# One joined product of the spectral convolution is summed as two again, and the list of jobs is laid out anew

## The chip, the cores and the metric

The kernel runs on one core of a Trainium2 chip. The core has a matmul engine (TensorE, PE in the profile), a vector engine (VectorE, DVE), an activation engine (ScalarE, ACT), a general engine (GpSimd, POOL), and a queue engine that issues transfers (SyncE, SP). Each engine works through its own instructions in program order and waits on semaphores for the others. The metric is the device time of one execution in microseconds (us); a time of several runs is their median.

## The reference

Two independent computations share the kernel. Half A is attention in a sliding, dilated window over 2048 positions, width 576, 32 heads of 18 channels, 8 keys per position with a distance of 2. Half B is a gated long convolution: a short filter over four taps of k, times v, then a causal convolution of length 2048 with one filter per channel, then times q.

```python
qkv = (x @ wqkv).reshape(B, S, 3, H, Dh)                  # A
logits = einsum("bhsd,bhswd->bhsw", q, k[idx]) * scale
o = einsum("bhsw,bhswd->bhsd", softmax(logits), v[idx])
a = o.reshape(B, S, D) @ wo
kv = (sum over t of k_pad[:, t:t+S] * shift_k[:, ks-1-t]) * v      # B
y = irfft(rfft(kv, 2S) * rfft(ssm_k, 2S))[:, :S] + kv * ssm_D
b = q * y
out = concatenate([a, b], axis=-1)
```

## The kernel before

Half B cuts the 2048 positions into four blocks of 512. Each block of kv (xw in the profile) and of the filter (Ks) is turned into a spectrum by matmuls with sine tables (jobs `x...`, line 682, and `K...`, lines 567 and 568). Output block j is the sum over i of 0 to j of the spectrum of input block i times the spectrum of filter block j - i. The channels are worked in thirds t of 192. A complex product is made in three real products on VectorE (job `pjti`, line 950, one instruction over 128 x 2304 elements) into one of five homes (`PHOMES`), and TensorE adds the products of one (j, t) up with identity matrices into PSUM (job `zjti`, line 975, sixteen 64 x 64 matmuls of 384 columns, in two accumulators r of eight). After the last term ScalarE copies both accumulators out (line 988); for the very last sum one of the two copies is VectorE's (line 986).

The signs with which TensorE adds depend on m = j - i alone, and those of m and m + 2 are opposite. For the thirds listed in `JOINED` a job `yjti` (line 958) therefore subtracts the product of i + 2 from that of i on VectorE, and the sum of i + 2 does not exist:

```python
gone = [(j, t, i + 2) for j, t, i in joined]
def join_products(n):
    tt(product_home(n), product_home(n), product_home(n + 2), ALU.subtract)
...
    if (j, t, i) not in gone:
        job(f"z{j}{t}{i}", spectral_sum, n)
    if (j, t, i) in joined:
        job(f"y{j}{t}{i}", join_products, n)
```

Then the inverse transform (jobs `i...`, line 1010; `b...` turns halves around, line 1059; the last piece of block 3, columns 384 to 575, is `i3384L`, lines 1029 and 1038), the gate by q (jobs `g...`, lines 1020 and 1075) and the store.

Half A has the projections (`q`, `k`, `v` jobs with unit numbers, lines 322 to 355, two parts a and b), the window's products (`L...`, VectorE, line 706) summed over a head's channels by TensorE (`G...`, line 720), the softmax (`sm...`), its weights spread by transfers (`D...`), times v (`V...`, VectorE, line 813), summed by TensorE (`A...`, lines 824 and 838), and the output projection (`O...`, lines 880 and 888).

Other names: `T` are the taps of a block (VectorE), `M` folds kv (line 545), `F` folds a filter block (line 602, copied out at line 605), `I` and `X5` small transposes (lines 397 and 428), `S1` and `Ex` work of ScalarE alone, `RG` copies of the weights of v (line 780), `N` one-row filter instructions on VectorE, `Tk3` forms the third part of filter block 3 by a transfer on SP and then an adding transfer on POOL (lines 634 and 626). Its target is the home of product `p212`, so it waits for `z212`, and `p300` waits for it.

The order of all of this is written out by hand: `ORDER` is a list of job names, and each engine sees its part of the jobs in this order. A quote mark at a name turns the parts of a job around, so that its small matmuls come first. Matmul results live in four pairs of PSUM banks (`banks`), handed out in turn and given back after the copy; the products of VectorE live in three homes for `L` and for `V` (`LHOMES`, `VHOMES`) and the five for `p`. A job that finds its bank pair or its home still in use waits.

The matmuls have five shapes on the array: 128 x 128 (most), 64 x 64 (`z`, `b`, `A` and the small matmuls of `O`), 64 x 128 (the small matmuls of the projections), 128 x 64 (`M`, `I`, `X5`, the units with last digit 4) and 128 x 32 (`G`). How often the shape changes along TensorE's row follows from the list.

Of the kernel before, what the change touches and what calls it, by code (L numbers as in the profile page):

```python
# [17 lines left out]
PSUM = bass.MemoryType.PSUM  # L18

ORDER = """  # L20
    T0 k03a' T1 S1 k03b I1 k02a k02b Lk2 Lv2 I0 k00a' Lk3 Lv3 M01 X5 k00b q10a Ex q10b Lf3 T2 Lo3 q13a' q13b
    k10a k10b T3 k13a' Lf2 k13b q12a q12b N2 Lo2 k01a M10 k01b Lf1 M00 k11a k11b q11a M11 q11b Lf0 N3 Lw SV L001
    k12a M20 k12b x001 M21 x021 q24a x020 q24b x000 Lo1 k24a Fr Lo0 Z2 N1 RG3 k24b RG2 F3 RG0 F2 L000 K310 G000
    K311 K210 K211 L002 K313 G001 RG4 F1 G002 L003 G003 K302 L004 G004 K301 L010 K212 L011 K303 K213 K203 N0 F0
    L012 K200 K300 G010 L013 K201 K312 K202 RG1 G011 G012 K113 K103 G013 L014 G014 K112 K102 K101 L100 K100 K010
    K111 K110 sm0a K001 K013 sm0b v24a' L101 v24b L102 G100 L103 G101 K012 sm0c sm0d U3 U2 K000 K011 K003 G102
    K002 D0 D1 v11a v11b G103 L104 G104 ak00 M30 v12a' v12b ak02 v01a ak01 L110 G110 M31 L111 G111 v01b v00a'
    L112 G112 L113 Wl v00b G113 x031 U1 L114 G114 V04 v10a' v10b A04 sm1a sm1b v02a v02b v03a' sm1c v03b x201
    V10 V11 sm1d V12 A10 v13a' v13b D2 x330 x310 x301 V13 A11 V20 V21 x200 x331 x230 x010 x221 A20 x321 V22 x210
    x011 V23 D3 V34 ax02 x220 x030 x300 D4 A21 V40 V41 A34 D5 O000' x211 V42 x320 x231 x111 x131 Tx2 A40 V43  # L30
    x120 x101 ax00 x130 ax01 V50 x121 x311 O001 A41 V51 O100' p000 x100 x110 O010 A50 V52 z000 O011' V53 O101
    A51 Tk2 p010 z010 ax10 O020' O021 p020 z020 O110' ak10 i000 p200 i02880 Q0 p100 z100 p101 p110 p111 Q1 z101
    i02881 i001 p121 p120 O111 z110 p201 z111 z120 p210 z121 O120 p211 z200 z210 z211 p212 z212 z201 p202 z202
    Tx3 p220 Tk3 p221 O030' p222 O121 b0288 z220 p301 z221 O031' p302 b00 z222 p303 i200 i100 g0 Q2 p300 y300
    p312 i12880 i201 i101 i12881 z300 z301 z303 p310 p311 y310 O130 b10 b1288 p313 g1 Q3 p322 O131' z310 p320
    z311 p321 z313 i22880 i300 b20 y320 p323 i22881 i301 b2288 g2 z320 z321 z323 b30 i3384L g30 g3384
"""

LHOMES = (0, 1, 2, 0, 1, 2, 0, 1, 2, 0, 1, 2, 0, 1, 0, 1, 0, 1, 0, 1)
VHOMES = (0, 1, 2, 0, 1, 2, 0, 1, 2, 0, 1, 2, 0, 1, 2, 0, 1, 2)  # L40
OHOMES = (0, 1, 1, 0, 2, 0, 1, 0)
JOINED = ("300 310 320").split()
PHOMES = (0, 1, 2, 3, 0, 1, 2, 3, 0, 4, 1, 2, 3, 0, 4, 1, 2, 3, 0, 1, 2, 3, 0, 1, 2, 3, 0, 1, 2, 3)


# [6 lines left out]
def kernel(  # L52
# [900 lines left out]
    acc = {}  # L953
    joined = [tuple(map(int, name)) for name in JOINED]
    gone = [(j, t, i + 2) for j, t, i in joined]
# [180 lines left out]
```

## Time and profile before

| | |
|---|---|
| median of three runs | 206.78 us (206.28, 206.78, 206.79) |
| the profiled execution | 206.3 us, with a span of 204.6 us |
| TensorE busy | 196.9 us (96%) |
| VectorE busy | 192.3 us (94%) |
| ScalarE busy | 155.6 us (76%) |
| granted clock of TensorE, mean | 0.994 |

The span runs from the first to the last instruction; 1.7 us of the time lie around it. A group in the profile names line, engine, instruction, target and sources, and gives the count, the busy time, the mean duration and the idle time before. "PE busy" of matmuls is drawn from modelled ends and covers short stalls; where a stall matters, the starts of matmuls are compared.

### The profile page before, as it was taken

Reading aid. Unit: us, or ns where it says so; the run is one execution under the profiler, and the core shown is the slowest. Engines: PE = TensorE matmul, PEld = TensorE weight load, DVE = VectorE, ACT = ScalarE, POOL = GpSimd, SP = SyncE. Lnnn points to the kernel's source line nnn. Section 1 sums busy time; section 2 is a strip of 40 time slices with the busy share of each in tenths; the row PEclk is TensorE's granted clock in tenths of the full one; section 3 lists DMA queues with packets and bytes.
Section 4 is the critical chain, followed back from the end, with each engine's and each line's share of the span. In section 5 each row is a group of like instructions: output and inputs, shape, how many; then the busy total and the mean of one; then the engine's idle time right before and its main releaser. Section 6 shows DMA issues by size and latency. Waiting matters only on the chain.

```text
span 204.6 us, 5004 instructions
## 1 busy us (share of the span) xinstructions
PE 196.9 (96%) x2074; PEld 109.9 (54%) x2074; DVE 192.3 (94%) x146; ACT 155.6 (76%) x223; POOL 60.8 (30%) x106
## 2 busy tenths in 40 slices
PE   7999999999989999999999999999999999999990
PEld 2543544334455646543245556776666767766660
DVE  7559999999999999999999999999999999899992
ACT  4788995678899999966578678886778767767760
POOL 8989500011348581400380000004090001030300
PEclk9999999999999999999999999999999999999997
DMA  6999899989509869999899990879989303944555
GB/s 197 280 293 306 175 289 373 214 177 281 169 3 146 111 82 185 167 180 222 157 235 216 248 244 34 141 183 334 186 227 233 100 28 122 227 130 145 153 182 150
DMA packets 34916, 38.48 MB, mean 188 GB/s; under 512 B 17523, under 2 KB 28911, under 8 KB 34894
## 3 DMA queue, kind: packets, MB, share of 16 engines
q1 hardware_dynamic: 26668, 24.29, 46.5%
q0 software_dynamic: 5760, 11.36, 29.5%
q10 hardware_dynamic: 2466, 2.51, 3.6%
q8 instruction: 16, 0.26, 0.5%
q14 instruction: 6, 0.05, 0.1%
HBM read 13.11 MB, written 4.72 MB: 87 GB/s over the span
## 4 chain that ended last, share of the span: by engine, by line
PE 88%; DMA 3%; ACT 2%; DVE 2%; issue 1%; SPq 1%; DVEq 0%
PE ps_proj L322 18%; PE ps_fx L682 8%; PE ps_wo L888 8%; PE ps_z L975 8%; PE ps_inv L1010 7%; PE ps_acc L824 7%; PE ps_fk L567 5%; PE ps_log L720 5%; DMA Ks<-in_A_x_dram 3%; PE ps_proj L333 3%; PE ps_proj L326 3%; PE ps_proj L439 3%; PE ps_fk L568 3%; PE ps_fold L545 2%; PE ps_wo L880 1%
## 5 line engine op out<-in xcount | busy, mean ns | idle before, releaser
L322 PE MATMUL ps_proj<-xw 128*128 128x512 bf16 x160 | 38.5, 380 | 0.0
L706 DVE TENSOR_TENSOR av<-qk 128x4096 bf16<-128x4096 bf16 (+1 forms) x16 | 31.7, 2014 | 0.1
L322 PEld LDWEIGHTS <-xw 128*128 128x128 bf16 x160 | 13.9, 98 | 19.4 <-issue 5.7
L988 ACT ACTIVATE av<-ps_z 128x768 bf16<-128x768 f32 x23 | 17.2, 811 | 6.5 <-PE ps_z L975 6.0
L517 DVE TENSOR_TENSOR tB<-kj,skb 128x4608 bf16<-128x4608 bf16 (+1 forms) x8 | 19.3, 2416 | 0.1
L950 DVE TENSOR_TENSOR qk<-xw,Ks 128x2304 bf16<-128x2304 bf16 x14 | 18.9, 1354 | 0.3 <-PE ps_z L975 0.3
L684 ACT ACTIVATE xw<-ps_fx 128x576 bf16<-128x576 f32 x32 | 18.6, 665 | 0.3 <-PE ps_fx L682 0.2
L618 ACT ACTIVATE Ks<-ps_fk 128x576 bf16<-128x576 f32 x32 | 18.6, 699 | 0.2 <-PE ps_fk L568 0.2
L355 ACT ACTIVATE qk<-ps_proj 128x1024 bf16<-128x1024 f32 x14 | 14.3, 1023 | 5.2 <-PE ps_proj L333 2.8
L888 PE MATMUL ps_wo<-qk 128*128 128x288 bf16 x128 | 17.9, 287 | 0.0
L626 POOL DMA_DIRECT2D Ks<-Ks x8 | 10.1, 1426 | 26.0 <-PE ps_back L1059 19.3
L682 PE MATMUL ps_fx<-xw,TB 128*128 128x288 bf16 x128 | 17.7, 287 | 0.0
L567 PE MATMUL ps_fk<-Ks,TB 128*128 128x384 bf16 x62 | 16.5, 327 | 0.1
L824 PE MATMUL ps_acc<-av,ident 64*64 64x512 bf16 x160 | 15.3, 378 | 0.0
L1010 PE MATMUL ps_inv<-av,TI 128*128 128x288 bf16 (+1 forms) x112 | 15.2, 292 | 0.0
L568 PE MATMUL ps_fk<-Ks,TB 128*128 128x192 bf16 x62 | 15.2, 246 | 0.0
L682 PEld LDWEIGHTS <-TB 128*128 128x128 bf16 x128 | 11.9, 98 | 5.9 <-issue 2.7
L888 PEld LDWEIGHTS <-qk 128*128 128x128 bf16 x128 | 11.7, 98 | 5.4 <-issue 2.7
L355 ACT ACTIVATE v<-ps_proj 128x1024 bf16<-128x1024 f32 x9 | 9.3, 1033 | 6.5 <-PE ps_proj L322 4.5
L813 DVE TENSOR_TENSOR av<-Ks,v 128x4096 bf16<-128x4096 bf16 x6 | 13.5, 2286 | 0.0
L827 ACT ACTIVATE qk<-ps_acc 128x1024 bf16<-128x1024 f32 x8 | 8.2, 1024 | 6.7 <-PE ps_acc L824 6.7
L1010 PEld LDWEIGHTS <-TI 128*128 128x128 bf16 x112 | 10.6, 98 | 4.2 <-issue 1.1
(195 smaller groups left out, 441.6 us busy)
## 6 DMA issues: line engine op xcount, KB each, us to landing
Ks<-Ks POOLq DMA_DIRECT2D x8, 576.0 KB, 7.8
TB<-av SPq DMA_DIRECT2D x12, 256.0 KB, 5.4
kj<-in_B_k_dram SPq DMA_DIRECT2D x6, 504.0 KB, 7.0
vt<-in_B_v_dram SPq DMA_DIRECT2D x8, 288.0 KB, 5.3
Ks<-av SPq DMA_DIRECT2D x8, 256.0 KB, 5.6
out_dram<-qk ACTq DMA_DIRECT2D x5, 288.0 KB, 3.7
Ks<-in_A_x_dram SPq DMA_DIRECT2D x2, 576.0 KB, 5.4
xw<-in_A_wqkv_dram SPq DMA_DIRECT2D x2, 576.0 KB, 6.2
```

Of the source, the lines that this page charges most:

```text
L322: nc.tensor.matmul(ps[:, jp, :], wq(kb, comp, 128 * ct, 128), xT(kb, 1024 * jj + 512 * jp, 512), **se)
L355: nc.scalar.activation(view(t, o + pad + 1024 * jj, [[512, 2], [1, 512]]), ps[:], ACT.Copy)
L517: tt(to, view(kj, row * D, [[D, n], [D, 4], [1, D]]), view(skb, row * D, [[D, n], [0, 4], [1, D]]), ALU.mult)
L567: nc.tensor.matmul(o[:, 0:2], w, rhs[:, 0:2], start=start, stop=stop)
L568: nc.tensor.matmul(o[:, 2], w, rhs[:, 2], start=start, stop=stop)
L618: nc.scalar.activation(view(Ks, k_at(m, cs ^ (m & 1)) + 96 * gi, [[768, 3], [384, 2], [1, 96]]), acc3(ps), ACT.Copy, scale=(PSG, MSG)[cs][ ...
L682: nc.tensor.matmul(ps[:, pm, 0:HD], TX[:, 2 * pm + c, 128 * gi:128 * gi + 128], kv[:, 2 * c + pm, HD * h:HD * h + HD], start=(c == 0), sto ...
L706: tt(view(P, at, [[step, 4], [256, nj], [1, 256]]), view(t, o + 256 * hh, [[0, 4], [512, nj], [1, 256]]), view(tk, ok + 2 + 8 * ug + 256 * ...
L824: nc.tensor.matmul(acc[64 * o:64 * o + 64, h, :], ident[64 * h:64 * h + 64, 64 * h:64 * h + 64], view(P[s], 256 * u, [[2048, 2], [1, 256]] ...
L888: nc.tensor.matmul(ps[:, r, 0:HD], oT(hh, j + 2 * r, t)[:, o:o + 128], wo[:, t // 2, t % 2, HD * h:HD * h + HD], start=(t == 0 and not fli ...
L950: tt(product_home(n), view(xw, HB * XG[i] + QTR * t, [[HB, 3], [1, QTR]]), view(Ks, k_at(j - i, 0) + QTR * t, [[HB, 3], [1, QTR]]), ALU.mult)
L1010: nc.tensor.matmul(ps[:, c, 0:n], TI[:, sl, pm, 128 * c:128 * c + 128], Yall(j % 2, pm, sl, slice(c0, c0 + n)), start=(pm == 0 and sl == 0 ...
```

## The change

`JOINED` loses its third entry. In the last third (t = 2) of output block 3 there is no job `y320` any more; instead the sum `z322` is a job of its own. `ORDER` is written anew from end to end: the same jobs otherwise, in other places, with the quote marks at other names. Homes and everything else stay.

```diff
--- before.py
+++ after.py
@@ -18,28 +18,28 @@
 PSUM = bass.MemoryType.PSUM
 
 ORDER = """
-    T0 k03a' T1 S1 k03b I1 k02a k02b Lk2 Lv2 I0 k00a' Lk3 Lv3 M01 X5 k00b q10a Ex q10b Lf3 T2 Lo3 q13a' q13b
-    k10a k10b T3 k13a' Lf2 k13b q12a q12b N2 Lo2 k01a M10 k01b Lf1 M00 k11a k11b q11a M11 q11b Lf0 N3 Lw SV L001
-    k12a M20 k12b x001 M21 x021 q24a x020 q24b x000 Lo1 k24a Fr Lo0 Z2 N1 RG3 k24b RG2 F3 RG0 F2 L000 K310 G000
-    K311 K210 K211 L002 K313 G001 RG4 F1 G002 L003 G003 K302 L004 G004 K301 L010 K212 L011 K303 K213 K203 N0 F0
-    L012 K200 K300 G010 L013 K201 K312 K202 RG1 G011 G012 K113 K103 G013 L014 G014 K112 K102 K101 L100 K100 K010
-    K111 K110 sm0a K001 K013 sm0b v24a' L101 v24b L102 G100 L103 G101 K012 sm0c sm0d U3 U2 K000 K011 K003 G102
-    K002 D0 D1 v11a v11b G103 L104 G104 ak00 M30 v12a' v12b ak02 v01a ak01 L110 G110 M31 L111 G111 v01b v00a'
-    L112 G112 L113 Wl v00b G113 x031 U1 L114 G114 V04 v10a' v10b A04 sm1a sm1b v02a v02b v03a' sm1c v03b x201
-    V10 V11 sm1d V12 A10 v13a' v13b D2 x330 x310 x301 V13 A11 V20 V21 x200 x331 x230 x010 x221 A20 x321 V22 x210
-    x011 V23 D3 V34 ax02 x220 x030 x300 D4 A21 V40 V41 A34 D5 O000' x211 V42 x320 x231 x111 x131 Tx2 A40 V43
-    x120 x101 ax00 x130 ax01 V50 x121 x311 O001 A41 V51 O100' p000 x100 x110 O010 A50 V52 z000 O011' V53 O101
-    A51 Tk2 p010 z010 ax10 O020' O021 p020 z020 O110' ak10 i000 p200 i02880 Q0 p100 z100 p101 p110 p111 Q1 z101
-    i02881 i001 p121 p120 O111 z110 p201 z111 z120 p210 z121 O120 p211 z200 z210 z211 p212 z212 z201 p202 z202
-    Tx3 p220 Tk3 p221 O030' p222 O121 b0288 z220 p301 z221 O031' p302 b00 z222 p303 i200 i100 g0 Q2 p300 y300
-    p312 i12880 i201 i101 i12881 z300 z301 z303 p310 p311 y310 O130 b10 b1288 p313 g1 Q3 p322 O131' z310 p320
-    z311 p321 z313 i22880 i300 b20 y320 p323 i22881 i301 b2288 g2 z320 z321 z323 b30 i3384L g30 g3384
+    T0 k03a k00a k00b S1 Lk2 k03b k01a' k01b I0 Lv2 M00 X5 T1 Lk3 T2 Lv3 T3 I1 Lf3 Lo3 Lf2 q24a Lo2 N3 N2 Ex
+    q10a q10b k11a' k11b Lf1 q13a' q13b k12a' k12b q11a' q11b M01 q24b M11 k02a k02b M10 SV k13a k10a' k13b M20
+    k10b L000 q12a' q12b Lf0 x001 L001 x020 Lo1 x021 M21 x000 Lw RG2 RG3 Lo0 Fr k24a' N1 k24b Z2 F3 F2 K312 K310
+    K211 L002 K212 RG4 G000 G001 K311 L003 RG0 N0 G002 L004 L010 K313 F1 G003 K301 G004 L012 L011 K302 K210 K203
+    K200 K300 K303 F0 G010 K213 K201 K202 L013 G011 L014 G012 RG1 K111 K110 G013 G014 K103 L100 K101 K102 K112
+    K011 K010 K113 sm0a sm0b L101 L102 K100 v24a v24b G100 G101 L103 K013 sm0c sm0d K001 G102 L104 K012 K002
+    K003 K000 ak00 ak01 U3 U2 v00a' G103 L110 G104 L111 x031 v00b v01a v12a v01b ak02 G110 G111 L112 L113 v11a'
+    v11b Wl v12b G112 D0 L114 M31 G113 V04 x010 G114 sm1a v10a D1 v10b V11 A04 V10 sm1b v02a v02b v03a' sm1c
+    v03b x220 x201 sm1d V12 x211 A10 M30 V13 D2 V20 U1 v13a' v13b A11 V21 x301 D3 x311 x331 V22 x330 x011 A20
+    V23 x300 x230 x321 x310 x210 D4 V34 A21 V41 x030 V40 x231 D5 A34 V42 x320 x200 x221 x120 x130 x100 A40 V43
+    Tx2 O000' x111 x110 O001 ax02 Tk2 A41 ax00 O100' ax01 x131 x121 V50 x101 O010 V51 A50 p000 z000 V52 O011'
+    O101 V53 A51 p010 Q0 z010 ax10 O020' O021 p020 z020 ak10 p200 Q1 p100 O110' i000 i02880 z100 p101 z101 p111
+    i001 p120 p110 i02881 O111 z110 z111 z120 p121 z121 p201 p210 p211 O120' Tx3 z200 p212 z210 z211 z212 Tk3
+    p202 z201 p220 z202 p221 p222 O030' O121 b00 z220 p301 z221 z222 O031' b0288 p302 p303 i100 g0 i12880 p300
+    i200 i101 i201 Q2 i12881 y300 z300 b10 p312 p310 z301 b1288 p311 z303 b20 O130' O131 y310 z310 z311 p313
+    z313 g1 Q3 p323 i22880 p321 i300 i22881 i301 p320 p322 z320 b2288 g2 z321 z322 z323 b30 i3384L g30 g3384
 """
 
 LHOMES = (0, 1, 2, 0, 1, 2, 0, 1, 2, 0, 1, 2, 0, 1, 0, 1, 0, 1, 0, 1)
 VHOMES = (0, 1, 2, 0, 1, 2, 0, 1, 2, 0, 1, 2, 0, 1, 2, 0, 1, 2)
 OHOMES = (0, 1, 1, 0, 2, 0, 1, 0)
-JOINED = ("300 310 320").split()
+JOINED = ("300 310").split()
 PHOMES = (0, 1, 2, 3, 0, 1, 2, 3, 0, 4, 1, 2, 3, 0, 4, 1, 2, 3, 0, 1, 2, 3, 0, 1, 2, 3, 0, 1, 2, 3)
 
 
```

## The prediction

> **What bounds the kernel now.** I read the busy shares and the chain of the page first, then busy time by stage, then the starts on the VectorE row.
>
> ```profile
> span 204.6 us, 5004 instructions
> PE 196.9 (96%) x2074; PEld 109.9 (54%) x2074; DVE 192.3 (94%) x146; ACT 155.6 (76%) x223; POOL 60.8 (30%) x106
> ...
> PE 88%; DMA 3%; ACT 2%; DVE 2%; issue 1%; SPq 1%; DVEq 0%
> ```
>
> TensorE and VectorE are both nearly full, and the chain that ended last runs over TensorE. The table by stage (columns: busy us of PE, PEld, DVE, ACT, POOL, each with its count, then clock, DMA share and GB/s):
>
> ```profile
> 17.80:58.80 41.00, 41.00 (x291) 18.30 (x291) 40.27 (x27) 33.17 (x45) 9.39 (x19) 1.00 0.93 225
> 58.80:88.40 29.60, 28.84 (x279) 16.43 (x278) 29.46 (x20) 29.51 (x47) 16.90 (x16) 1.00 0.82 127
> 88.40:167.60 79.20, 79.03 (x954) 46.21 (x952) 78.72 (x53) 58.14 (x83) 13.54 (x17) 1.00 0.82 189
> 167.60:197.40 29.80, 29.53 (x437) 20.07 (x437) 28.65 (x23) 21.14 (x32) 5.13 (x7) 1.00 0.53 151
> ```
>
> From 17.8 on no stage has a free engine among these two: VectorE lacks 0.5 us of 79.2 in the third row, TensorE 0.2. From 58.8 to 88.4 (the filter units `K`) ScalarE is full as well, 29.51 of 29.60. Only the last row leaves VectorE 1.15 us. Where these waits are:
>
> ```profile
> 162.24 1.36 DVE L950 TENSOR_TENSOR v<-xw,Ks 128x2304 bf16<-128x2304 bf16 x1 [0.21 <-PE ps_z L975]
> ...
> 169.13 1.36 DVE L950 TENSOR_TENSOR v<-xw,Ks 128x2304 bf16<-128x2304 bf16 x1 [0.33 <-PE ps_z L975]
> ...
> 176.00 1.36 DVE L950 TENSOR_TENSOR qk<-xw,Ks 128x2304 bf16<-128x2304 bf16 x1 [0.25 <-PE ps_z L975]
> ...
> 179.03 1.36 DVE L950 TENSOR_TENSOR av<-xw,Ks 128x2304 bf16<-128x2304 bf16 x1 [0.41 <-DMA Ks<-Ks]
> ```
>
> These are `p201`, `p220`, `p303` and `p300`. Three wait for a home that TensorE has yet to read, one for a transfer. So the two engines run in lock-step, each a few tenths behind the other, and a gain on one alone goes into waits for the other.
>
> **The terms.** From the chain (start, us, what) and from the VectorE row:
>
> ```profile
> 48.47 0.60 PE ps_fx L682 x4
> ...
> 118.60 2.56 PE ps_fx L682 x20
> ...
> 145.08 0.65 PE ps_z L975 x16
> ```
>
> ```profile
> 185.63 1.35 DVE L958 TENSOR_TENSOR av<-av,qk 128x2304 bf16<-128x2304 bf16 x1
> 186.90 1.35 DVE L950 TENSOR_TENSOR qk<-xw,Ks 128x2304 bf16<-128x2304 bf16 x1
> ```
>
> *Taken out:* `y320`, one instruction like that at 185.63 (`y310`). The next begins 1.27 us later, so VectorE gets 1.27 us less.
> *Put in:* `z322`, sixteen 64 x 64 matmuls. Such a set took 0.65 us, so TensorE gets 0.65 us more. ScalarE has the same two copies after t = 2, later by what the sum is later. No transfer is added or taken out.
> *Moved:* everything. What the list itself tells is how often TensorE changes its tile shape. Sixteen more matmuls of one shape took 2.56 - 0.60 = 1.96 us, 0.1225 each; four alone should take 0.49 and took 0.60, so a stay in one shape costs 0.11 us beside its matmuls. Going through both lists with the shapes of each job I count 122 changes before and 113 after (with the one at the start, where `k03a` has lost its quote mark), nine fewer: -1.0 us. Whole row of TensorE: 0.65 - 1.0 = -0.35 us. Whole row of VectorE: -1.27 us. Which part of either reaches the end has to be read stage by stage.
>
> **Up to the end of the first softmax's sums.** Six of the nine saved changes stand ahead of `G014` (53 against 47). They would bring TensorE 0.65 us ahead, but `G014` needs the product `L014`:
>
> ```profile
> 74.80 3.41 DVE L706 TENSOR_TENSOR av<-qk 128x2048 bf16<-128x2048 bf16 x2
> ```
>
> ```profile
> 76.15 0.60 PE L720 MATMUL ps_log<-av,E 128*32 128x512 bf16 x8
> ```
>
> `L014` begins at 74.80 and runs over 2048 columns, `L100` behind it over 4096; a third of 3.41 is 1.14, so it ends near 75.94. `G014` began at 76.15. In the new list the same VectorE instructions stand ahead of `L014` (four `T`, four `N`, nine `L`), and VectorE had no wait there. So `G014` can come 0.1 us earlier at best, whatever is saved ahead of it. That also holds for a stall that goes:
>
> ```profile
> 60.36 0.61 PE L720 MATMUL ps_log<-av,E 128*32 128x512 bf16 x8 [0.62 <-DVE av L706]
> ```
>
> `G000` waited 0.62 us for `L000`, which stood behind `L001` and `N1`; in the new list `L000` is first and its sum comes later. What is late next is `G002` (behind `L002`), then `G004`, then `G014`. I cost this part at 0; its cover is VectorE's full row. `RG0` moved behind `K311` shifts one copy inside a stage that ScalarE fills either way: 0. On the queues SP's transfers keep their sequence, on POOL `Lo0` goes ahead of `Fr` and `Z2` behind the pad transfer of `k24b`; the first product to need them, `N0`, and the v units come us later: 0.
>
> **From `G014` on.** Three changes fewer (69 against 66) and `z322` more: 0.65 - 0.33 = +0.32 us on a TensorE row that, by the third row of the table, has 0.2 us free in 79. Inside this row two `x` units come ahead of `A40` and `O000` goes behind it; the sum stays.
>
> VectorE's 1.27 us lie behind `y310`. What comes ahead is the same work in nearly the same sequence, and the end is tied to it by a chain that the change leaves alone:
>
> ```profile
> 167.58 0.36 PE L975 MATMUL ps_z<-Ks,ident 64*64 64x384 bf16 x4 [0.17 <-DVE Ks L950]
> ```
>
> ```profile
> 168.47 0.47 SPq L634 DMA_DIRECT2D Ks<-Ks  x1
> ```
>
> ```profile
> 173.00 1.21 POOL L626 DMA_DIRECT2D Ks<-Ks  x1 [19.30 <-PE ps_back L1059]
> ```
>
> `z212` at 167.58 had waited 0.17 us for `p212`; when it has read its home, the transfers of `Tk3` go (168.47, 173.00), and `p300` began when they had landed, at 179.03. From there `p300 y300 p312 p310 p311 y310` follow, unchanged, and `z310` at 187.03 (below) came 0.13 after the end of `y310` (186.90 above). So by VectorE `z310` moves only by what `p212` moves: earlier by the waits ahead of it that shrink, at most 0.48 us (79.20 - 78.72, third row), later by what TensorE's +0.32 lets it wait in addition. By TensorE it moves by +0.32. In the old run the two met within 0.2 us at `z212`, so I take the later one.
>
> **The tail** of the chain:
>
> ```profile
> 187.03 2.14 PE ps_z L975 x48
> ...
> 191.56 0.37 PE ps_back L1059 x8
> ...
> 194.69 1.80 PE ps_z L975 x40
> ...
> 197.38 1.50 PE ps_inv L1029 x16
> ```
>
> From `z310` to the last inverse 10.35 us. The new list adds `z322` (+0.65), moves `b20` out of it to the small matmuls of `O130` (-0.25, of 0.37 with its 0.11), and has two changes fewer (-0.22): +0.18, all of it inside the +0.32 above. VectorE's share: `p323 p321 p320 p322 g2` in place of `p322 p320 p321 y320 p323 g2`, so it is through 1.27 us sooner and the last products are no longer waited for; but TensorE has its own contiguous 10 us there, and the last copies, the inverse, the gate and the store follow as before. Here the whole -1.27 is lost. It costs nothing that `p323` now stands ahead of three others: its home is free when `z313` is through, and `g1` covers that.
>
> **Sum.** 206.3 (profiled execution) + 0.65 - 0.33 + 0 for all ahead of `G014` = 206.6. The median of the runs shown lies 0.48 above the profiled execution, so the forecast for a median is 206.78 + 0.32 = 207.1. Less than 0.3% (0.62 us) is about what a measurement of this kernel cannot tell from no change, so I forecast: no change that can be told, on the slow side.
>
> **Rivals.**
> *Slower, by the start of ScalarE.* The first projection on the chain, and the row of ScalarE:
>
> ```profile
> 18.59 1.83 PE ps_proj L322 x8
> ```
>
> ```profile
> 19.33 1.99 ACT L382 ACTIVATE TB<-Ks 128x1024 bf16<-128x1024 int16 x2
> 21.23 1.01 ACT L355 ACTIVATE qk<-ps_proj 128x1024 bf16<-128x1024 f32 x1
> ...
> 33.03 1.02 ACT L355 ACTIVATE qk<-ps_proj 128x1024 bf16<-128x1024 f32 x1 [1.03 <-PE ps_proj L333]
> ```
>
> Now the second sine (`S1`) comes straight after the first, which ends near 20.3. In the new list it stands behind the copy of `k00b`. Three sets of four matmuls (`k03a k00a k00b`, 0.9 each by the first row) and a tail end near 21.5, an estimate, so ScalarE idles 1.2 us. Within the next 2 us `I0 M00 X5 I1 q24a` ask for six pairs of banks, of which there are four, and wait for its copies. TensorE then reaches `F3` not 0.65 early but some 0.5 late (1.2 - 0.65), and ScalarE, full from 58.8 to 88.4, passes on most of it; `G014` would be 0.45 late. Against it: ScalarE has holes of 1 us soon after (33.03) to make it good. It decides when `G014` is more than 0.3 late; then 0.45 + 0.32 = +0.8, 207.6.
> *Slower, by a home.* `V43` needs the home that `A40` reads. `ax02`, a third of a 1.35 us instruction, 0.45, has gone from ahead of `V40` to behind `V43`, so `V43` needs `A40` that much sooner; if TensorE is not sooner, VectorE waits 0.45 us, and `p212`, `Tk3` and the end go with it: +0.32 + 0.45 = +0.8, 207.6. It decides if `A40` begins no earlier than in the old run. Against: all waits of VectorE from 88.4 to 167.6 made up 0.5 us before.
> *Faster, VectorE sets the pace all along.* Then TensorE follows in its shadow, `p212` gains up to 0.5 and the tail the rest of 1.27: 206.78 - 1.27 = 205.5. For it: in the first three rows of the table VectorE lacks 0.7, 0.1 and 0.5 us. Against: in the last 30 us TensorE has 0.27 us free and VectorE 1.15. It decides if the tail from `z310` on shrinks. The Trainium skill, Perfetto Trace Analysis, Identifying the Most-Contended Engine, says to optimize the engine with the highest occupancy and warns that matmul busy time is no good measure for TensorE; by that rule VectorE at 94% would be that engine and the change a gain of 1.27 us. The starts of the matmuls speak against it in the tail and do not decide it before.
>
> **How the numbers follow.** No change that can be told 0.45; slower by ScalarE's start 0.24; slower by a home or another new wait 0.15; faster 0.16. Range: 206.1 (part of the gain on VectorE kept, 0.7) to 208.3 (both slow cases, 0.32 + 0.45 + 0.45 = 1.2, and 0.3 for a wait that I do not see); the likeliest case alone is 206.5 to 207.4.
>
> **What would show it.** Right: VectorE 1.27 us less busy, TensorE's `z` matmuls sixteen more; `G014` within 0.3 of 76.15; `p300` 11.4 us after `z212`; `z310` to the last inverse 10.3 to 10.6 us; VectorE idle in the tail. Wrong: `z310` more than 0.6 away from 187.3, or holes of ScalarE at 20 us that TensorE repeats at `q24a`.

## The result, and the profile after

The median went from 206.65 us (206.02 to 207.19, 13 runs) to 207.92 us (207.27 to 209.26, 13 runs). The ratio is 1.007, with a 95% interval of 1.005 to 1.009: slower by 1.0 to 1.9 us. One execution of this study, the traced one of the kernel with `b20` moved, took 229.25 us at a granted clock of 0.852 and is left out. The range of the prediction holds it, its likeliest case (no change that can be told) does not.

The profiled execution of after took 209.26 us, the slowest of its thirteen, against 206.28 for that of before, one of the faster. So the two traces differ by 3 us where the medians differ by 1.3, and the first task is to see what of the 3 us belongs to the kernel. The page of after, the rows that answer to those shown of before:

```profile
span 207.5 us, 5032 instructions
...
PE 198.7 (96%) x2090; PEld 111.9 (54%) x2090; DVE 191.5 (92%) x145; ACT 155.3 (75%) x223; POOL 61.6 (30%) x106
...
PE 83%; ACT 5%; DMA 4%; DVE 4%; issue 1%; DVEq 0%; ACTq 0%
```

Sixteen matmuls more (2074 to 2090) and one VectorE instruction less (146 to 145), as announced. In the chain ScalarE, VectorE and transfers have 13% in place of 7%. By stage, same columns as before:

```profile
17.80:58.80 41.00, 40.28 (x282) 17.73 (x281) 40.38 (x26) 31.57 (x43) 9.41 (x23) 1.00 0.89 222
58.80:88.40 29.60, 28.86 (x278) 16.32 (x276) 27.38 (x20) 29.54 (x47) 16.84 (x19) 1.00 0.75 112
88.40:167.60 79.20, 79.20 (x920) 46.05 (x923) 78.27 (x52) 59.38 (x86) 14.25 (x18) 1.00 0.85 194
167.60:197.40 29.80, 29.08 (x440) 20.53 (x440) 28.00 (x22) 20.69 (x32) 5.11 (x7) 1.00 0.49 137
```

In the first stage (which in this execution holds some of the preamble) TensorE lacks 0.72 us where it lacked nothing, and ScalarE got through 1.6 us less work (33.17 to 31.57). In the second VectorE, full before, lacks 2.2 us. Both point to the same place, the stretch up to the first softmax.

**What belongs to the single execution.** The first transposes of the preamble, in before and in after (start, us, engine, line):

```profile
5.03 1.07 PE L410 MATMUL ps_x<-ident,Ks 128*128 128x128 bf16 x16
...
18.00 0.38 PE L441 MATMUL ps_proj<-xw 64*128 64x512 bf16 x1
```

```profile
5.44 1.91 PE L410 MATMUL ps_x<-ident,Ks 128*128 128x128 bf16 x16
...
18.94 0.60 PE L441 MATMUL ps_proj<-xw 64*128 64x512 bf16 x2
```

The same sixteen matmuls took 1.07 us in one execution and 1.91 in the other, ahead of anything that the change touches: from start to start 56 ns in before, 107 ns in after. The last matmul of the preamble began at 18.00 and at 19.17 (the second of the pair at 18.94). Over the thirteen traces of this study it began between 17.74 and 19.17: from 17.74 to 18.87 in five kernels with the old start of the list, from 18.35 to 19.17 in eight with the new. The medians speak for chance: what they differ from before, less the difference in the table below, is -0.1 us on average for the eight and 0.0 for three of the others, though single kernels lie from -0.6 to +0.6. Chance is argued by this, not shown: at least eleven of the sixteen transposes ran at the slow rate in all eight traces with the new start, and in only one of five with the old. The Trainium skill, TensorE: Matmul & The Clock Gate, Part 1: The HAM clock gate, says that TensorE begins at half its clock, and that the window after which it is released runs free of the kernel, so that the transition comes at another time in each run. The two rates of these transposes agree with it; in the trace of the split alone the step goes from 107 to 56 ns within the sixteen. It gives 500 ns to either side for the transition; the start of the list moved by 1.4 us here, in which waits for transfers have a share.

So I count from the last matmul of the preamble. Worked out from the starts of matmuls, in us (kernels are named below; the copy, an adding transfer and `p300` lie in the fourth column; `L` is the last inverse, line 1029):

| kernel | to `F3` | `F3` to `G014` | `G014` to `z200` | `z200` to `z310` | `z310` to `L` | all |
|---|---|---|---|---|---|---|
| before | 37.89 | 20.26 | 89.15 | 21.74 | 10.34 | 179.38 |
| after | 38.49 | 20.41 | 89.41 | 22.41 | 10.44 | 181.16 |
| split only | 37.89 | 20.27 | 89.15 | 21.75 | 10.85 | 179.91 |
| order only | 38.49 | 20.42 | 89.27 | 21.83 | 13.52 | 183.53 |
| old start | 37.89 | 20.82 | 89.41 | 21.91 | 10.44 | 180.47 |
| new start | 38.49 | 20.58 | 89.15 | 21.67 | 10.26 | 180.15 |
| old to softmax | 37.89 | 20.30 | 89.27 | 21.81 | 10.44 | 179.72 |
| sine early | 38.49 | 20.43 | 89.27 | 22.12 | 10.44 | 180.76 |
| sum early | 38.49 | 20.67 | 89.27 | 21.98 | 10.44 | 180.85 |
| home | 38.49 | 20.42 | 89.13 | 22.47 | 10.44 | 180.95 |
| I1 moved | 38.62 | 20.39 | 89.27 | 22.85 | 10.44 | 181.58 |
| I1 and RG2 moved | 38.62 | 20.40 | 89.27 | 21.78 | 10.42 | 180.50 |
| b20 and g1 moved | 37.89 | 20.30 | 89.15 | 22.12 | 10.35 | 179.81 |

But for the fourth, the columns repeat to a few hundredths, at most 0.14 us, where the list is the same, far finer than the medians. After loses 0.60 up to `F3`, 0.15 more up to `G014`, 0.1 to 0.26 up to `z200`, 0.67 in the fourth column (which moves from run to run), and 0.10 in the tail.

### The profile page after: what moved, and what is told of

Same layout as the page of the kernel before. It is cut to its first block, busy times and chain, and to the rows that moved or that the text cites. A ratio compares the mean times of both kernels' runs of the same rounds, so it can differ in the third digit from the quotient of the medians.

```text
span 207.5 us, 5032 instructions
## 1 busy us (share of the span) xinstructions
PE 198.7 (96%) x2090; PEld 111.9 (54%) x2090; DVE 191.5 (92%) x145; ACT 155.3 (75%) x223; POOL 61.6 (30%) x106
## 4 chain that ended last, share of the span: by engine, by line
PE 83%; ACT 5%; DMA 4%; DVE 4%; issue 1%; DVEq 0%; ACTq 0%
PE ps_proj L322 18%; PE ps_fx L682 7%; PE ps_acc L824 7%; PE ps_wo L888 7%; PE ps_z L975 6%; PE ps_fk L567 6%; PE ps_log L720 5%; PE ps_inv L1010 4%; PE ps_proj L439 3%; DMA Ks<-Ks 3%; PE ps_proj L333 3%; PE ps_fk L568 3%; PE ps_proj L326 2%; PE ps_fold L545 2%; PE ps_sk L453 2%
## 5 line engine op out<-in xcount | busy, mean ns | idle before, releaser
L618 ACT ACTIVATE Ks<-ps_fk 128x576 bf16<-128x576 f32 x32 | 20.1, 775 | 0.3 <-PE ps_fk L568 0.3
L626 POOL DMA_DIRECT2D Ks<-Ks x8 | 10.9, 1639 | 25.9 <-PE ps_z L975 19.4
```

Of the source, the lines that this page charges most:

```text
L618: nc.scalar.activation(view(Ks, k_at(m, cs ^ (m & 1)) + 96 * gi, [[768, 3], [384, 2], [1, 96]]), acc3(ps), ACT.Copy, scale=(PSG, MSG)[cs][ ...
```

## The experiments

Edits are shown against the kernel named; times and ratios are always against before.

**The two halves of the change.** First the split alone, against before:

```diff
-    z311 p321 z313 i22880 i300 b20 y320 p323 i22881 i301 b2288 g2 z320 z321 z323 b30 i3384L g30 g3384
+    z311 p321 z313 i22880 i300 b20 p323 i22881 i301 b2288 g2 z320 z321 z322 z323 b30 i3384L g30 g3384
...
-JOINED = ("300 310 320").split()
+JOINED = ("300 310").split()
```

> The list of before, with y320 taken out and z322 put in behind z321; nothing else moves. Theory (TensorE sets the pace in the last 10 us, VectorE waits for it): the 0.65 us of z322 show whole and the 1.27 us of y320 bring nothing: 206.65 + 0.65 = 207.3, ratio 1.003. Rival (VectorE sets the pace): 206.65 - 1.27 = 205.4, ratio 0.994.

Measured: 206.80 us against 206.58, ratio 1.0014 (0.9998 to 1.003); the tail 10.85 us, 0.51 more. The gate `g2` and what stands ahead of it on VectorE:

```profile
193.30 1.35 DVE L950 TENSOR_TENSOR qk<-xw,Ks 128x2304 bf16<-128x2304 bf16 x1
195.80 1.36 DVE L1075 TENSOR_TENSOR TB<-v,TB 128x2304 bf16<-128x2304 bf16 x1 [1.15 <-ACT v L1065]
```

The 1.27 us that VectorE saves come back as a wait of 1.15 us for ScalarE's copy of turned halves (L1065). That copy comes right behind one for which ScalarE had waited 0.65 us for TensorE's inverse. The rival (VectorE sets the pace, 0.994) is out: the split alone gains nothing and costs at most what `z322` adds.

Then the order alone, the join kept; against after, as are all that follow up to the tail:

```diff
-    z313 g1 Q3 p323 i22880 p321 i300 i22881 i301 p320 p322 z320 b2288 g2 z321 z322 z323 b30 i3384L g30 g3384
+    z313 g1 Q3 p323 i22880 p321 i300 i22881 i301 p320 p322 y320 z320 b2288 g2 z321 z323 b30 i3384L g30 g3384
...
-JOINED = ("300 310").split()
+JOINED = ("300 310 320").split()
```

> The list of after, with y320 put back behind p322 and z322 taken out. Theory (the loss is in the new order and lies ahead of the tail): after less z322, 207.92 - 0.65 = 207.3, ratio 1.003. Rival (the loss is in the split): the order alone gains what the shape changes save, 206.65 - 0.33 = 206.3, ratio 0.998. If VectorE's subtraction is what ends last in the new tail, up to 1.27 more than after: 209.2, ratio 1.012.

Measured: 210.10 us, ratio 1.018 (1.0154 to 1.0207), above all that was expected. Up to `z200` it is as after to 0.14 us; the tail is 13.52 us. `z320` on TensorE:

```profile
197.63 0.36 PE L975 MATMUL ps_z<-av,ident 64*64 64x384 bf16 x4 [2.12 <-DVE av L958]
```

In the new tail `p323 p321` come first on VectorE and `p320 p322` last, so a subtraction placed behind them makes TensorE wait 2.12 us. The new tail and the split belong together; this kernel says nothing on the order ahead of the tail that the next ones do not say better.

**The start and the filter stage.** The first 73 jobs of before (`T0` to `L000`, with `RG0`) in front of the list of after; against after:

```diff
-    T0 k03a k00a k00b S1 Lk2 k03b k01a' k01b I0 Lv2 M00 X5 T1 Lk3 T2 Lv3 T3 I1 Lf3 Lo3 Lf2 q24a Lo2 N3 N2 Ex
...
-    k10b L000 q12a' q12b Lf0 x001 L001 x020 Lo1 x021 M21 x000 Lw RG2 RG3 Lo0 Fr k24a' N1 k24b Z2 F3 F2 K312 K310
-    K211 L002 K212 RG4 G000 G001 K311 L003 RG0 N0 G002 L004 L010 K313 F1 G003 K301 G004 L012 L011 K302 K210 K203
+    T0 k03a' T1 S1 k03b I1 k02a k02b Lk2 Lv2 I0 k00a' Lk3 Lv3 M01 X5 k00b q10a Ex q10b Lf3 T2 Lo3 q13a' q13b
...
+    k12a M20 k12b x001 M21 x021 q24a x020 q24b x000 Lo1 k24a Fr Lo0 Z2 N1 RG3 k24b RG2 F3 RG0 F2 L000 K312 K310
+    K211 L002 K212 RG4 G000 G001 K311 L003 N0 G002 L004 L010 K313 F1 G003 K301 G004 L012 L011 K302 K210 K203
```

And the first 72 jobs of after (`T0` to `F2`) and `RG0` in front of the list of before; its last lines against before:

```diff
-    k12a M20 k12b x001 M21 x021 q24a x020 q24b x000 Lo1 k24a Fr Lo0 Z2 N1 RG3 k24b RG2 F3 RG0 F2 L000 K310 G000
+    k10b L000 q12a' q12b Lf0 x001 L001 x020 Lo1 x021 M21 x000 Lw RG2 RG3 Lo0 Fr k24a' N1 k24b Z2 F3 F2 RG0 K310
+    G000 ...
```

> The list of after from K312 on, behind the first 73 jobs of before (T0 to L000, with RG0 among them). Theory (the start on ScalarE makes TensorE late, and VectorE then waits for G000): most of the loss goes, 206.65 + 0.32 = 207.0, ratio 1.002 or less; G014 within 0.3 of 76.15 when the preamble is like that of before. Rival (the filter stage or what is behind it): as after, ratio 1.006 to 1.007.

> The list of before from K310 on, behind the first 72 jobs of after (T0 to F2) and RG0; y320 joined as before. Theory (the start): 206.65 + 0.9 = 207.5, ratio 1.004 or more, with VectorE waiting at L002 or L003 for G000 or G001. Rival (the rest): no change, ratio 0.999 to 1.001.

Measured: old start 207.72 us, ratio 1.0052 (1.0033 to 1.0071), so most of the loss stayed; new start 207.13 us, ratio 1.0032 (1.0017 to 1.0046), so the start alone loses too (VectorE's waits come at `L004` and `L010`, not at `L002` or `L003`). The two theories are not alternatives. Up to `G014` (first two columns) before takes 58.15 us, the old start with the new filter stage 58.71, the new start with the old filter stage 59.07, and both new 58.90. Each alone costs 0.6 to 0.9, and together no more.

Both taken back, the list of before up to `sm0a` and that of after behind it; the seam against after:

```diff
-    ... G012 RG1 K111 K110 G013 G014 K103 L100 K101 K102 K112 K011 K010 K113 sm0a sm0b L101 L102 K100 v24a v24b G100 ...
+    ... G011 G012 K113 K103 G013 L014 G014 K112 K102 K101 L100 K100 K010 K111 K110 sm0a K011 sm0b L101 L102 v24a v24b G100 ...
```

> The list of before up to sm0a (start and filter stage), the list of after from there on. Theory (each of the two, start and filter stage, costs 0.5 to 0.7 us up to G014 and together no more; what is left is 0.2 for V43's home, 0.1 in the z sums, 0.1 in the tail): G014 58.1 us after the start of the list, as in before; ratio 1.002 to 1.003. Rival (the order behind the softmax loses as much): 1.006.

Measured: 207.12 us, ratio 1.0028 (1.0009 to 1.0047), and 58.19 us up to `G014`. So about 0.0042 of after's 0.0070, or 0.9 us, uncertain by some 0.6, lies ahead of the first softmax (0.75 by the table), and the rest behind it.

**Where the start loses.** TensorE in after, from 25 us on:

```profile
25.83 0.64 PE L397 MATMUL ps_ti<-ident,TB 128*64 128x128 bf16 x16
26.30 0.66 PE L545 MATMUL ps_fold<-xw,fold 128*64 128x288 bf16 x8
27.01 0.42 PE L428 MATMUL ps_x<-ident,Ks 128*64 128x128 bf16 x8
27.99 0.64 PE L397 MATMUL ps_ti<-ident,TB 128*64 128x128 bf16 x16 [0.55 <-ACT TI L401]
```

`I0 M00 X5` take all four pairs of banks (`M00` takes two), and `I1` waits for ScalarE's copy of `I0`. The prediction laid this to the idle time of ScalarE ahead of `S1`. So `S1` was moved to where ScalarE has nothing to do:

```diff
-    T0 k03a k00a k00b S1 Lk2 k03b k01a' k01b I0 ...
+    T0 k03a S1 k00a k00b Lk2 k03b k01a' k01b I0 ...
```

> The list of after with S1 moved from behind k00b to behind k03a; nothing else. Theory (ScalarE's hole at 22 us is what makes TensorE late): TensorE no longer waits 0.55 us at I1, F3 comes 0.5 us sooner after k03a (38.18 us in after), G014 0.5 sooner after k03a (58.6 in after), ratio 1.004 to 1.005. Rival (ScalarE's backlog of copies at F3 and the filter stage set the pace, not the hole): F3 earlier, G014 still 58.5 to 58.6 us after k03a, ratio 1.007.

Measured: 207.59 us, ratio 1.0071 (1.0045 to 1.0097); 38.49 us to `F3`, as in after to the hundredth. ScalarE's row ahead of the burst, and the wait:

```profile
25.48 1.02 ACT L355 ACTIVATE qk<-ps_proj 128x1024 bf16<-128x1024 f32 x1 [1.02 <-PE ps_proj L322]
26.40 1.08 ACT L401 ACTIVATE TI<-ps_ti 128x512 bf16<-128x512 f32 x2
```

```profile
27.53 0.64 PE L397 MATMUL ps_ti<-ident,TB 128*64 128x128 bf16 x16 [0.55 <-ACT TI L401]
```

The idle time only moved: ScalarE now waits 1.02 us for `k01b`, and from there on everything is as it was. The hole at `S1` costs nothing. Neither theory named the cause rightly: F3 did not even come sooner.

Then the burst itself:

```diff
-    X5 T1 Lk3 T2 Lv3 T3 I1 Lf3 Lo3 Lf2 q24a Lo2 N3 N2 Ex q10a q10b k11a' ...
+    X5 T1 Lk3 T2 Lv3 T3 Lf3 Lo3 Lf2 q24a Lo2 N3 N2 Ex q10a q10b I1 k11a' ...
```

> The list of after with I1 moved from behind T3 to behind q10b, so that I0 M00 X5 I1 no longer stand in one row; nothing else. Theory 1 (the burst of short jobs, each with a pair of banks and a copy of ScalarE, makes TensorE wait at I1, and this is carried to the end): from the end of the preamble to F3 37.8 us (38.49 in after), to G014 58.3 (58.90), ratio 1.004. Theory 2 (F3 comes sooner, but ScalarE's backlog of copies there takes it back): to F3 37.8, to G014 58.8 to 58.9, ratio 1.007.

Measured: 208.25 us, ratio 1.0079 (1.0047 to 1.011); 38.62 us to `F3`, 0.13 later than in after where both theories had it 0.7 sooner.

```profile
27.42 0.84 PE L326 MATMUL ps_proj<-xw 128*64 128x512 bf16 x6 [0.55 <-ACT TI L401]
```

The same 0.55 us, now at `q24a`. Three short jobs in a row (`I0 M00 X5`; two of them 0.5 and 0.7 us from start to start) are enough: `I0` and `M00` have copies of 1.1 and 1.2 us on ScalarE, and whatever comes fourth waits. So the wait follows the burst. That the loss up to `F3` goes when the three stand apart was not tried.

**The filter stage.** In addition to `I1`, `RG2` was moved behind `k24b`'s copy, for which `F2` seemed to wait:

```diff
-    M21 x000 Lw RG2 RG3 Lo0 Fr k24a' N1 k24b Z2 F3 F2 K312 K310 ...
+    M21 x000 Lw RG3 Lo0 Fr k24a' N1 k24b Z2 RG2 F3 F2 K312 K310 ...
```

> As the kernel with I1 moved, and RG2 moved from ahead of k24b's copy to behind Z2, so that F2 does not wait for that copy behind two weight copies. Theory 1: to F3 37.8, K310 3.3 us after F3 (3.98 in after), to G014 58.1 as in before, ratio 1.003. Theory 2 (ScalarE has that work to do in the filter stage either way): to G014 58.8, ratio 1.007.

Measured: 207.97 us, ratio 1.0066 (1.0041 to 1.0091); from `F3` to `K310` 3.99 us, as in after (3.98), and 59.02 up to `G014`. Theory 2 for the stretch behind `F3`: the wait only went from `F2`, which had waited 0.27 us for `k24b`'s copy in after, to the first two filter units. ScalarE has its copies to make one way or the other. What it has there in after:

```profile
56.83 2.51 ACT L780 ACTIVATE xw<-Ks 128x576 bf16<-128x576 bf16 x2
59.19 1.07 ACT L355 ACTIVATE qk<-ps_proj 128x1024 bf16<-128x1024 f32 x1
60.09 2.34 ACT L605 ACTIVATE Ks<-ps_rev 128x576 bf16<-128x576 f32 x4
62.21 2.39 ACT L618 ACTIVATE Ks<-ps_fk 128x576 bf16<-128x576 f32 x4
```

The starts follow each other without a gap. In before these four `F` copies (L605) stood at 58.12 and 60.33 between others; in after they begin at 60.09. The first filter unit on TensorE comes 3.38 us behind `F3`, in before 2.95.

VectorE's part was tested by the place of `G000`. In after (rows of VectorE):

```profile
59.65 2.27 DVE L706 TENSOR_TENSOR v<-qk 128x4096 bf16<-128x4096 bf16 x1
63.98 2.29 DVE L706 TENSOR_TENSOR av<-qk 128x4096 bf16<-128x4096 bf16 x1 [2.05 <-PE ps_log L720]
```

`L003` needs the home of `L000`, and so `G000`, which now stands behind `K312 K310 K211 K212`.

```diff
-    Z2 F3 F2 K312 K310 K211 L002 K212 RG4 G000 G001 K311 ...
+    Z2 F3 G000 F2 K312 K310 K211 L002 K212 RG4 G001 K311 ...
```

> The list of after with G000 moved ahead of F2 (it stands behind K312 K310 K211 K212 in after); nothing else. Theory 1 (VectorE's 2.05 us wait at L003 for G000's home carries the loss to G014): the wait shrinks below 0.5 us and G014 comes 0.5 us or more sooner, ratio 1.004. Theory 2 (TensorE is paced by ScalarE's copies in the filter stage, VectorE's wait is only a symptom): VectorE waits at L013 for G010 instead, G014 stays 58.6 us after k03a, ratio 1.007.

Measured: 208.06 us, ratio 1.0094 (1.0067 to 1.0122), no faster than after; 59.16 up to `G014`.

```profile
68.87 4.50 DVE L706 TENSOR_TENSOR av<-qk 128x4096 bf16<-128x4096 bf16 x2 [1.12 <-PE ps_log L720]
73.58 2.29 DVE L706 TENSOR_TENSOR v<-qk 128x4096 bf16<-128x4096 bf16 x1 [0.22 <-PE ps_log L720]
```

The wait of 2.05 us is gone from `L003`, and 1.34 us of it came back at `L012` and `L013`, which wait for later sums. Theory 2: in after VectorE's wait is a symptom; `G014` begins 0.58 us behind the end of `L014` there (estimated as in the prediction). Where TensorE is not late (old start), the same place of `G000` makes VectorE wait 0.69 us at `L003`:

```profile
62.86 2.29 DVE L706 TENSOR_TENSOR av<-qk 128x4096 bf16<-128x4096 bf16 x1 [0.69 <-PE ps_log L720]
```

That is near the loss of that kernel up to `G014` (0.56), and its `G014` follows the end of `L014` by 0.12 us. That the wait causes the loss there is read from the trace; no edit tested it.

**Behind the softmax: a home.** In after `V43` waits, where in before it did not (the first row holds two instructions, `V42` and `V43`; before, then after):

```profile
132.38 4.49 DVE L813 TENSOR_TENSOR av<-Ks,v 128x4096 bf16<-128x4096 bf16 x2
```

```profile
136.24 2.29 DVE L813 TENSOR_TENSOR av<-Ks,v 128x4096 bf16<-128x4096 bf16 x1 [0.23 <-PE ps_acc L824]
```

```diff
-    V34 A21 V41 x030 V40 x231 ... A40 V43 Tx2 O000' x111 x110 O001 ax02 Tk2 ...
+    V34 A21 V41 x030 ax02 V40 x231 ... A40 V43 Tx2 O000' x111 x110 O001 Tk2 ...
```

> The list of after with ax02 back ahead of V40; nothing else. Theory (V43 waits 0.23 us for the home that A40 reads, and p020 carries it on): no wait at V43, z020 8.0 us or less after z000 (8.22 in after, 7.91 in before), ratio 1.006. Rival (the wait is made up by slack behind it): z020 as in after, ratio 1.007. If ax02 stands in the way of V40 there: z000 later by up to 0.47.

Measured: the wait is gone, `z020` comes 7.90 us after `z000`, and `G014` to `z200` takes 89.13 us, what before takes. But the time is 208.60 us, ratio 1.011 (1.0086 to 1.0134): not better than after. What `z200` gained did not arrive behind it: in this profile `p300` waited 0.98 us for the transfer into its home. The single trace is 0.21 us shorter than that of after from the preamble to `L`, so why the median is higher stays open.

**The transfer ahead of `p300`.** That wait differs between kernels whose list around it is the same; the two ends, from the kernels with `I1` moved, and with `I1` and `RG2` moved:

```profile
181.73 1.36 DVE L950 TENSOR_TENSOR av<-xw,Ks 128x2304 bf16<-128x2304 bf16 x1 [1.37 <-DMA Ks<-Ks]
```

```profile
180.86 1.36 DVE L950 TENSOR_TENSOR av<-xw,Ks 128x2304 bf16<-128x2304 bf16 x1 [0.22 <-DMA Ks<-Ks]
```

From `z212` to `p300` it took 11.4 to 12.5 us in nine kernels with the new order there, 11.80 on average, and 11.2 to 11.5 in four with the old. Most of this is the adding transfer (L626): from its issue to its landing it took 6.0 us in before, 6.5 in after, and 7.4 and 6.1 in the two kernels above. Whether the new order slows the transfers or whether this is chance with single traces stays open.

**Can the tail give more?** The new tail without `z322` takes 10.44 - 0.65 = 9.79 us, 0.55 less than the old one; by the prediction's sum that is `b20`, which is out of it, and two shape changes. So in before, joined, `b20` was moved, and then `g1` as well:

```diff
-    ... y310 O130 b10 b1288 p313 g1 Q3 p322 O131' z310 p320 z311 p321 z313 i22880 i300 b20 y320 p323 i22881 ...
+    ... y310 O130 b10 b1288 b20 p313 g1 Q3 p322 O131' z310 p320 z311 p321 z313 i22880 i300 y320 p323 i22881 ...
```

> The list of before with b20 moved from behind i300 to behind b1288, out of the tail, two shape changes less. Theory 1 (TensorE alone sets the pace from z310 on): tail from z310 to the last inverse 10.34 - 0.45 = 9.9 us, ratio 0.998. Theory 2 (VectorE's row ties it too: p323 ends 0.1 us ahead of z323 in before): z323 waits for p323, tail 10.3, ratio 1.000.

```diff
-    ... b10 b1288 b20 p313 g1 Q3 p322 O131' z310 p320 z311 p321 z313 i22880 i300 y320 p323 i22881 ...
+    ... b10 b1288 b20 p313 Q3 p322 O131' z310 p320 z311 p321 z313 i22880 i300 y320 p323 g1 i22881 ...
```

> As the kernel with b20 moved in the list of before, and g1 moved behind p323, so that p323 comes 1.27 us sooner on VectorE. Theory 1 (only p323 tied the tail to VectorE): tail 9.9, ratio 0.998. Theory 2 (VectorE's row is full up to its copy for z323, which ends last either way): tail 9.9 to 10.3 and the end where it was, ratio 1.000. If g1's later store is what ends last: 1.003.

Measured: 206.64 us against 206.35, ratio 1.0006 (0.9987 to 1.0024), for `b20` alone, of which only the times are known. That speaks for theory 2. In before VectorE's row has no gap over 0.04 us from `p300` to its copy for `z323`; its end:

```profile
194.50 1.35 DVE L950 TENSOR_TENSOR qk<-xw,Ks 128x2304 bf16<-128x2304 bf16 x1
195.77 1.35 DVE L1075 TENSOR_TENSOR TB<-v,TB 128x2304 bf16<-128x2304 bf16 x1
197.04 0.95 DVE L986 CAST av<-ps_z 128x768 bf16<-128x768 f32 x1
```

`p323` (194.50 and 1.35 long) ends just ahead of `z323` at 195.97. With `g1` moved as well the kernel became slower: 208.03 us, ratio 1.0075 (1.0048 to 1.0102).

```profile
196.83 1.36 DVE L1075 TENSOR_TENSOR TB<-v,TB 128x2304 bf16<-128x2304 bf16 x1 [1.48 <-ACT v L1065]
198.11 0.95 DVE L986 CAST av<-ps_z 128x768 bf16<-128x768 f32 x1
```

That is more than any of its theories allowed for. Now `g2` waits 1.48 us and stands ahead of the copy that the last inverse needs. The wait begins on ScalarE: the copy of `i301` writes the home that `g1` reads, so it waits for the moved `g1`, and the copy that `g2` needs (L1065) comes behind it.

```profile
195.45 0.81 ACT L1013 ACTIVATE v<-ps_inv 128x768 bf16<-128x768 f32 x1 [2.05 <-DVE TB L1075]
```

TensorE did gain: from `z310` to `z323` it took 8.39 us, in before 8.94. But that gain was lost behind `z323`, so this kernel does not tell whether a tail without `b20` can be faster when `g1` is out of the way. No version of this study beats before.

## Why the prediction was right in its range and wrong in its likeliest case

*The terms.* Right. `z322` adds sixteen matmuls; VectorE loses one instruction. (Its busy time fell by 0.8 us, 192.3 to 191.5, and not by 1.27; the difference is not explained.) The six shape changes saved ahead of `G014` are all ahead of `F3` (39 to 33, from the list) and count: with 6 x 0.11 = 0.66 us saved and 0.60 lost, TensorE waited some 1.2 us more on that stretch than in before, most of it at the burst. The changes saved behind it lie behind `z200`.

*Up to `G014`: costed at 0, measured +0.75 us.* This is the step that failed. "Its cover is VectorE's full row" says nothing on a loss, and there was no slack for one. TensorE's waits at the burst (0.55) and for the copies at the filter stage were not in the sum but in a rival. The cover itself was misread too. In the kernel with the split alone, whose list is the same up to there, VectorE had a hole:

```profile
65.58 2.29 DVE L706 TENSOR_TENSOR v<-qk 128x4096 bf16<-128x4096 bf16 x1 [0.44 <-PE ps_log L720]
```

Yet `G014` came at the same place, 58.17 us behind the preamble in place of 58.15, and 0.45 behind the end of `L014` (estimated in the same way). So VectorE's row alone does not hold `G014` in the old list; whether a gain of TensorE would have arrived was not tested. `G014` came 1.92 us later than 76.15, of which 1.17 is the preamble of that execution:

```profile
78.07 0.60 PE L720 MATMUL ps_log<-av,E 128*32 128x512 bf16 x8
```

*The rival by ScalarE's start.* Its place was right and its size for `G014`, +0.45, was too small: +0.75. Of its two halves the hole at `S1` is refuted (nothing changed when it was taken away), for the reason that the prediction gave against it: ScalarE has holes soon after. The other half, short jobs in a row asking for banks, is what the trace shows. What it missed is the filter stage: in after ScalarE's copies bunch up at `F3`, and behind the old start the new filter stage loses 0.56 by another way, VectorE's wait at `L003`.

*The stall of `G000`.* That it costs 0 when it goes was right: in the kernel with the split alone, by the chance of that execution, `G000` came 0.7 us sooner and `G001` at the same place (63.28 against 63.23). That another wait takes its place was foreseen for `G002`, `G004`, `G014`; it was `L003`, on VectorE, that waited, and where the start was old that is, by the trace, the loss.

*The rival by a home.* Right in mechanism: `V43` waits for `A40`. Half the price: 0.23 us in place of 0.45, and 0.14 to 0.28 up to `z200`.

*From `G014` on, +0.32.* The sum was about right for the wrong reasons: 0.1 to 0.26 is the home, the tail is +0.10 (predicted +0.18), and the fourth column, +0.05 to +1.1, was not in it. By the medians, the kernel with the split and the new order behind the softmax alone lost 0.2 to 1.0 us.

*The chain over `Tk3`, 11.4 us.* Mis-sized for the new order: 12.09 in the profile of after, 11.80 on average. Not explained.

*The tail.* Right: 10.44 us (predicted 10.3 to 10.6), and VectorE's -1.27 is lost there, most of it as a wait of 1.09 at `g2`:

```profile
198.53 1.36 DVE L1075 TENSOR_TENSOR TB<-v,TB 128x2304 bf16<-128x2304 bf16 x1 [1.09 <-ACT v L1065]
```

*Faster, VectorE sets the pace.* Out. The rule of the Trainium skill, Perfetto Trace Analysis, Identifying the Most-Contended Engine, would have had the 94% engine relieved; it was, and the split alone brought +0.3 us (0.0 to 0.6). What fits better is the section Optimization Strategy of the same page of the Trainium skill, which says that the most-contended engine can change over time within a kernel. The traces agree: here ScalarE's copies around 27 and 60 us, a home of VectorE at 136, TensorE in the tail.

*Sum.* 0.75 up to `G014`, 0.1 to 0.26 up to `z200`, 0.4 on average between `z200` and `z310` (mean of nine kernels, 22.13, less 21.74), 0.10 in the tail: 1.35 to 1.5 us. The medians differ by 1.27. By its own signs of being wrong the likeliest case is out: `z310` came at 189.89, 1.69 us later than in before when both preambles are taken off. That the result still lies in the range is in part luck, because one slow case was larger than its price, the other smaller, and the transfers were in neither.

## What to carry to other kernels

In this kernel two engines are full in lock-step. VectorE's saving in the tail was worth nothing by itself, but a loss that began at the copies of a third engine reached the end: a full row of one engine is no cover against losses, and each new row of short jobs has to be counted in copies of the engine that empties their banks. Where single executions differ by more than the effect, compare intervals between two instructions behind the part that varies; four of the five columns repeated to a few hundredths, at most 0.14 us, where the medians were uncertain by 0.4. A tail is written for its own work: the same order lost 3 us as soon as one instruction was put back into it.

## What was not expected of the hardware

The preamble's last matmul began anywhere from 17.74 to 19.17 us, with the first transposes at 1.07 to 1.91 us for the same sixteen matmuls, while the granted clock reads 1.00 in every stretch of the preamble too. And the copy and adding transfer from `z212` to `p300` took 11.2 to 12.5 us from trace to trace, for the same two transfers.
